# Norm weights folded into the conversion of the feed-forward weights, rows scaled on ScalarE

## The chip, the cores and the metric

The kernel runs on one core of a Trainium2 chip. The metric is the device time of one execution in microseconds (us). The core has five engines, each with a queue of its own that it works off in order: TensorE (PE: matmuls and transposes), VectorE (DVE), ScalarE (ACT), GpSimd (POOL) and SyncE (SP), which here issues the DMAs. An instruction waits at the head of its queue until what it needs is there, and all behind it wait with it.

## The reference

Three stages follow each other. An attention with exponential gates over 2 batches, 8 heads and 768 steps with heads of 40 gives x of 1536 tokens x 320. Then a normed and gated feed-forward layer, then a second feed-forward layer:

```python
def _moe_ref(x, w_gate, w_val, w_out, rms_g):      # 320 -> 1536 -> 320
    rms = np.sqrt(np.mean(x * x, axis=-1, keepdims=True) + 1e-06)
    xn = x / rms * rms_g
    g = xn @ w_gate
    silu = g * (1.0 / (1.0 + np.exp(-g)))
    val = xn @ w_val
    return silu * val @ w_out

def _moe2_ref(x, w_in, w_out):                     # 320 -> 2048 -> 320
    h = x @ w_in
    g = np.maximum(0.01 * h, h)
    return g @ w_out
```

The weights of both layers are 64-bit floats in memory. The kernel reads their bits and makes of each weight a value rounded to the matmul's format and a rest, and multiplies with both.

## The kernel before

The order of all work is one long string, `ORDER`, of some 3000 tokens such as `xn.5` or `a.10`; `play` calls for each the function of that name, and the instructions that it issues go to the ends of the engines' queues. No scheduler changes that order. Only the tokens that the change touches matter here:

- Attention works on 12 tiles T of 128 tokens (6 chunks of 128 steps of each of 2 batches). `dq.T` (`ld_qk`) loads queries and keys in two halves of 40 rows each, `de.T` (`ld_e`) a decay row, spread over 40 rows per half. `arg.T.e` is four exponentials of 128x128 on ScalarE (L359), `y1`, `rec`, `yr` form the attention's output y on VectorE.
- The norm of a tile: `sq.T` (L478) squares y on ScalarE and sums each row; `y2.T.0` (L485) divides by 320 and adds epsilon on VectorE; `y2.T.1` (L487) raises it to -1/2 on GpSimd; `y2.T.2` (L489 to L491) is a Newton step on VectorE in three operations on one column. `xn.T` (`att_xna`, L496) multiplies y by this column and by the norm weights, `gb`, a 128x320 tile into which a DMA spreads the 320 weights. `xc.T` (L500) copies the last 64 columns beside it on ScalarE, `tp.T` (L507) transposes on TensorE, `xh.T` (L511, ScalarE) rounds the result into X, `xl.T` (L515, VectorE) keeps the rest.
- The weights: `wA`, `wR`, `wB` load raw bits; the generators `weight_a`, `weight_r`, `weight_b` are taken a step further by each token `a.k`, `r.k`, `b.k`. The first step makes two halves of the number (L548 on VectorE, L550 on ScalarE), the second puts them together (L552, VectorE) and rounds on ScalarE (L573: 128x512 of key A, L616: two of 64x256 of key R, L627 and L628 of key B), the third takes the difference on VectorE (L575, L619, L630 and L631). Keys A.0 to A.11 and R.0 to R.5 belong to `w_gate` and `w_val`, later ones to the second layer.
- The feed-forward: `U` (L658) is the matmuls of gate `g` and value `v`, `T` the tanh (L685) or, once the attention is over, the silu (L683, with a table load before its first use), `E` (L690) and `M` multiply, `S` and `L` (L706, L712) split the product.
- `close` ends the attention's memory after `tp.11`; keys 8 to 11 of the weights use that memory and are converted only then.

VectorE's `V`, ScalarE's `A`, GpSimd's `G` and SyncE's `Q` are the engines in the code.

Of the kernel before, what the change touches and what calls it, by code (L numbers as in the profile page):

```python
# [50 lines left out]
id.1 id.1 id.1 id.1 z.0 z.1 z.2 did cr id.1 id.1 dfg dig id.1 id.1 id.1 wR.1 dq.0 ms id.1 sf.0.1 sa.0.1 ah sf.1.2 id.1  # L51
sa.1.2 wA.0 co.0.0.1 cv.0.0.1 cl z.3 z.4 z.5 r.1 fa.0.0 arg.0.0 sf.2.6 fa.1.1 uv.0.1 arg.1.1 fa.0.1 sa.2.6 uv.1.2
ux.0.1 co.1.0.1 wR.0 ug.2.6 id.1 co.0.1.2 arg.0.1 r.1 r.0 r.1 r.0 id.1 dn.2 dA.0.2 dq.1 r.0 ev.1.2 ux.2.6 ex.1.2 r.0
r.1 a.0 dn.1 cv.1.0.1 fa.1.0 arg.1.0 dn.0 th.0 eg.2.6 k.0 da.2 ex.2.6 a.0 k.1 qk.0 p.0.0 qk.1 a.0 p.1.0 av.0.0 p.0.1
av.0.1 abs.0 p.1.1 av.1.0 av.1.1 da.3 id.1 mask.2.1 cv.0.1.2 mask.2.0 co.0.2.6 dE.1.2 y1.0 id.1 arg.2.0 a.0 kv.0 abs.1
# [5 lines left out]
co.1.2.6 cv.1.2.6 xl.1 cb.1 y2.2.1 y2.2.2 r.3 qk.4 eq.3 av.3.1 inn.3 dv.1.2 xn.2 arg.4.0 xc.2 tp.2 abs.3 r.3 r.3 c.3
rec.3 dn.5 kv.3 a.4 xh.2 arg.4.1 xl.2 U.0.1.1 p.4.0 k.5 y1.3 da.5 a.4 st.3 U.0.1.0 cb.3 p.4.1 th.5 T.0.1 dn.4 th.4
mask.5.0 wA.3 yr.3 sq.3 a.4 E.0.1 mask.5.1 a.3 arg.5.1 dc.2.6 de.4 r.3 arg.5.0 y2.3.0 a.3 eq.4 M.0.1 av.4.0 av.4.1
inn.4 dq.5 qk.5 y2.3.1 y1.4 p.5.1 U.0.0.0 p.5.0 T.0.0 E.0.0 dv.2.6 U.0.0.1 M.0.0 da.6 mask.6.1 arg.6.1 de.5 wB.0 abs.4
dq.6 a.3 rec.4 mask.6.0 av.5.0 av.5.1 S.0.1 eq.5 y2.3.2 yr.4 S.0.0 inn.5 kv.5 abs.5 b.0 xn.3 rec.5 b.0 sq.4 y2.4.0
y2.4.1 arg.6.0 qk.6 L.0.1 p.6.1 U.0.2.0 p.6.0 U.0.2.1 T.0.2 E.0.2 c.2 y1.5 dq.7 b.0 c.5 st.5 qk.7 yr.5 y2.4.2 c.4 cb.5
sq.5 a.3 k.4 kv.4 id.1 xc.3 tp.3 xh.3 y2.5.0 y2.5.1 dq.8 xn.4 da.7 xc.4 M.0.2 wB.2 U.0.3.0 st.4 cb.4 y2.5.2 c.6 L.0.0
xn.5 xl.3 tp.4 xh.4 xl.4 U.0.3.1 S.0.2 xc.5 T.0.3 tp.5 xh.5 de.6 dn.6 av.6.0 E.0.3 xl.5 av.6.1 wB.3 M.0.3 L.0.2 eq.6
inn.6 abs.6 wA.5 b.0 b.3 U.1.0.0 T.1.0 E.1.0 U.1.0.1 M.1.0 U.1.1.0 da.8 U.1.2.0 b.3 mask.7.0 arg.7.0 p.7.0 dn.7 av.7.0
mask.7.1 arg.7.1 p.7.1 av.7.1 k.7 S.0.3 b.2 L.0.3 de.7 b.2 eq.7 S.1.0 b.2 inn.7 L.1.0 b.2 b.3 b.3 wB.4 rec.6 T.1.2  # L70
# [1039 lines left out]
```

## Time and profile before

| what | value |
|---|---|
| three timed runs | 443.22, 443.83, 448.07 us (median 443.83) |
| the profiled execution | 444.82 us, its span 443.0 us |
| busy: TensorE, VectorE, ScalarE, GpSimd | 429.1 (97%), 367.9 (83%), 280.7 (63%), 104.5 us (24%) |
| mean granted TensorE clock | 0.973 of full speed |
| chain that ended last | TensorE 83%, VectorE 8%, ScalarE 4%, DMA 2% |
| DMA | 42.14 MB, 95 GB/s over the span |

The span is the time from the first to the last instruction of one profiled execution; its own time includes what lies around. The busy shares are averages over stages with different limits; the first 75 us and the stretch from 155 to 175 us, where the change lies, are read apart below.

### The profile page before, as it was taken

How to read it: one execution, taken by the hardware profiler on the slowest of the kernel's cores; microseconds unless marked ns; L12 is line 12 of the kernel's file. 1: busy time of each engine (PE TensorE's matmuls, PEld its weight loads, DVE VectorE, ACT ScalarE, POOL GpSimd, SP SyncE). 2: the span in 40 equal slices, each digit the busy share in tenths (PEclk: the TensorE clock that was granted, in tenths of full speed). 3: DMA queues.
4: the chain of work that ended last, by engine and by line, in shares of the span. 5: the costliest groups of instructions: out<-in, count | busy, mean ns of one | idle time of the engine just before them, and what ended most of it. 6: DMA issues, size and time to landing. Idle time of an engine off the chain costs nothing.

```text
span 443.0 us, 9728 instructions
## 1 busy us (share of the span) xinstructions
PE 429.1 (97%) x3702; PEld 409.6 (92%) x3704; DVE 367.9 (83%) x827; ACT 280.7 (63%) x708; POOL 104.5 (24%) x166
## 2 busy tenths in 40 slices
PE   8897989999999999999999999999999999999997
PEld 4775978999999989999999999999999999999996
DVE  7998999677787758969989999888679897988775
ACT  5777866674664377644565565987866676577442
POOL 4644462431212000463736210010101010110000
PEclk9559999999999999999999999999999999999999
...
GB/s 220 320 304 248 181 323 115 222 169 115 223 2 78 56 77 123 57 84 39 85 2 2 1 0 1 1 9 148 30 34 74 108 48 32 30 31 31 0 2 178
DMA packets 16119, 42.14 MB, mean 95 GB/s; under 512 B 2056, under 2 KB 4040, under 8 KB 16072
## 3 DMA queue, kind: packets, MB, share of 16 engines
...
q8 instruction: 29, 0.48, 0.4%
q14 instruction: 18, 0.15, 0.1%
...
## 4 chain that ended last, share of the span: by engine, by line
PE 83%; DVE 8%; ACT 4%; DMA 2%; issue 2%; SPq 0%; DVEq 0%; ACTq 0%
PE h L808 13%; PE xa L730 10%; PE v L658 8%; PE g L658 8%; PE oa L981 6%; PE oa L979 6%; PE oa L980 6%; PE u L808 6%; PE xw L748 5%; PE h L814 3%; PE h L813 3%; PE s L343 2%; PE o L403 2%; PE u L813 1%; DMA Ab<-A_d 1%
## 5 line engine op out<-in xcount | busy, mean ns | idle before, releaser
L981 PE MATMUL oa<-wB,xl 128*128 128x320 f32 x192 | 59.3, 309 | 0.0
L980 PE MATMUL oa<-wB,xh 128*128 128x320 f32 x192 | 59.3, 309 | 0.0
L979 PE MATMUL oa<-wB,xh 128*128 128x320 f32 x192 | 59.3, 309 | 0.0
L658 PE MATMUL g<-X,wA 128*128 128x384 f32 x256 | 50.3, 341 | 1.8 <-DVE th L690 0.9
L991 DVE TENSOR_TENSOR x<-oa,x 128x320 f32<-128x320 f32 x84 | 39.5, 484 | 14.6 <-PE oa L981 13.9
L658 PE MATMUL v<-X,wA 128*128 128x384 f32 x256 | 49.9, 339 | 0.9 <-ACT X L511 0.7
L658 PEld LDWEIGHTS g<-X,wA 128*128 128x128 f32 x256 | 44.2, 188 | 3.9 <-DVE th L690 1.2
L658 PEld LDWEIGHTS v<-X,wA 128*128 128x128 f32 x256 | 44.5, 188 | 1.5 <-ACT X L511 0.8
L730 PE MATMUL xa<-sh,wB 128*128 128x384 f32 x160 | 45.9, 337 | 0.0
L590 POOL TENSOR_TENSOR sums<-w_A 128x128 f32<-128x128 f32 x8 | 3.9, 487 | 151.6 <-DVE w_A L552 147.0
L981 PEld LDWEIGHTS oa<-wB,xl 128*128 128x128 f32 x192 | 36.1, 188 | 0.1
L980 PEld LDWEIGHTS oa<-wB,xh 128*128 128x128 f32 x192 | 36.0, 188 | 0.0
L979 PEld LDWEIGHTS oa<-wB,xh 128*128 128x128 f32 x192 | 36.0, 188 | 0.0
L808 PE MATMUL h<-X,wA 128*128 128x384 f32 x144 | 32.2, 338 | 0.0
L730 PE MATMUL xa<-sl,wB 128*128 128x384 f32 x96 | 32.2, 336 | 0.0
L955 ACT ACTIVATE c<-c 128x384 f32<-128x384 f32 x48 | 25.2, 524 | 7.2 <-DVE c L852 3.4
L730 PEld LDWEIGHTS xa<-sh,wB 128*128 128x128 f32 x160 | 29.4, 188 | 0.1
L965 DVE TENSOR_TENSOR xl<-c,xh 128x384 fp32r<-128x384 f32 x48 | 26.0, 556 | 1.0 <-ACT xh L960 0.8
L960 ACT CAST xh<-c 128x384 fp32r<-128x384 f32 x48 | 24.3, 513 | 2.9 <-PE oa L980 2.2
L359 ACT ACTIVATE w<-Ab,aeu 128x128 f32<-128x128 f32 x80 | 25.3, 392 | 0.6 <-POOL Ab L363 0.6
L808 PEld LDWEIGHTS h<-X,wA 128*128 128x128 f32 x144 | 25.0, 188 | 0.1
L487 POOL TENSOR_TENSOR sm<-sm,mhalf 128x1 f32<-128x1 f32 x12 | 7.9, 661 | 66.5 <-DVE sm L485 66.5
...
## 6 DMA issues: line engine op xcount, KB each, us to landing
...
```

Of the source, the lines that this page charges most:

```text
L359: A.activation(w[:, j], src, AF.Exp, scale=-1.0, bias=col)
L658: PE.matmul(dst, a, x, start=(i == 0), stop=(i == len(seq) - 1))
L730: PE.matmul(xa, w, x, start=(k == 0), stop=(k == len(seq) - 1))
L748: PE.matmul(xas["w", g, i], a, x, start=(f == NE and k == 0), stop=(f == NF - 1 and k == len(seq) - 1),)
L808: PE.matmul(dst, x, y, start=first and j == 0, stop=j == 2, skip_group_check=not first)
L955: A.activation(t, src, AF.Prelu, alpha=0.01)
L960: A.copy(v["h"], v["t"])
L965: V.tensor_tensor(v["l"], v["t"], v["h"].bitcast(F32), op=ALU.subtract)
L979: PE.matmul(oa, v["h"][:, ts], wb[:, 0:DM], start=m == 0, stop=False)
L980: PE.matmul(oa, v["h"][:, ts], wb[:, DM:], start=False, stop=False)
L981: PE.matmul(oa, v["l"][:, ts], wb[:, 0:DM], start=False, stop=m == 1)
L991: V.tensor_tensor(dst, oas[k, p, i], dst, op=ALU.add)
```

## The change

The norm weights no longer multiply the tokens. Since the rows of `w_gate` and `w_val` meet the same 320 features, each weight row is multiplied by its norm weight when it is converted. A DMA early in SyncE's queue loads `gcol`, 128x3, the norm weights as columns (third column: the last 64, twice); the DMA into `gb` is gone.

- `xn.T` is one ScalarE instruction with the row's scale as a pointer to a column, at the same place of the order.
- The conversion of a key A to 11: the 128x512 rounding becomes two of 128x256, each with its column of `gcol` as scale, and the difference becomes two instructions of 128x256 that multiply and subtract. The pairs of keys R to 5 get the scale too, with no instruction more. Keys of the second layer are as before.
- y lives in three standing tiles of 128x321 whose last column holds epsilon's share; the square runs over 321 columns with a scale, so that its sum is the mean plus epsilon. `y2.T.0` is gone, and `y2.T.2` has two operations instead of three (signs in `rec` are turned for it).
- `ld_qk` and `ld_e` move 48 rows per half instead of 40: 24 DMAs of 192 instead of 160 KB, 20 of 96 instead of 80 KB.
- `A_hl` has room for two chunks (one is filled as before), which makes GpSimd's fill of it longer by 128 columns; three small fills for the epsilon columns stand beside it.

In the order only `dgb` has moved (to the start) and the `y2.T.0` have gone:

```diff
-id.1 id.1 id.1 id.1 z.0 z.1 z.2 did cr id.1 id.1 dfg dig id.1 id.1 id.1 wR.1 ...
+id.1 id.1 id.1 id.1 z.0 z.1 z.2 did cr id.1 id.1 dfg dig dgb id.1 id.1 id.1 wR.1 ...
...
-dA.2.6 eq.2 ux.1.2 co.1.1.2 cv.1.1.2 cv.0.2.6 sq.0 y2.0.0 yr.1 wA.2 kv.1 dgb p.2.0 ...
+... cv.0.2.6 sq.0 yr.1 wA.2 kv.1 p.2.0 ...
```

The code:

```diff
-    gb = attc.tile([128, DM], F32, name="gb")
+    gcol = const.tile([128, 3], F32, name="gcol")
+    Y = [attc.tile([128, DM + 1], F32, name=f"y{n}") for n in range(3)]
...
-        for r in (slice(0, D), slice(64, 64 + D)):
+        for r in (slice(0, 48), slice(64, 112)):
...
     def att_sq(T):
-        A.activation(junk, t["yf"], AF.Square, accum_out=t["sm"][:, 8:9])
+        A.activation(junk, t["yx"], AF.Square, scale=2.0 * DM ** -0.5, accum_out=t["sm"][:, 8:9])
     def att_y2(T, i):
-        if i == 0:
-            V.tensor_scalar(out=v_, in0=ss, scalar1=1.0 / DM, scalar2=1e-6, op0=ALU.mult, op1=ALU.add)
-        elif i == 1:
+        if i == 1:
             G.tensor_tensor(z, v_, mhalf, op=ALU.pow)
         else:
             V.tensor_scalar(out=z2, in0=z, scalar1=z, scalar2=v_, op0=ALU.mult, op1=ALU.mult)
-            V.tensor_scalar(out=z2, in0=z2, scalar1=-0.5, scalar2=1.5, op0=ALU.mult, op1=ALU.add)
-            V.tensor_tensor(z, z, z2, op=ALU.mult)
+            V.tensor_scalar(out=zn, in0=z2, scalar1=3.0, scalar2=z, op0=ALU.subtract, op1=ALU.mult)
     def att_xna(T):
-        V.scalar_tensor_tensor(out=xn[:, 0:DM], in0=t["yf"], scalar=t["z"], in1=gb, op0=ALU.mult, op1=ALU.mult)
+        A.activation(xn[:, 0:DM], t["yf"], AF.Copy, scale=t["z"])
     def memsets():
+        for y in Y:
+            G.memset(y[:, DM:], (DM * 1e-6) ** 0.5)
     def weight_a(key):
-        A.copy(w[:, 0:2], x)
+        for k in range(2):
+            A.activation(w[:, k], x[:, k], AF.Copy, scale=gcol[:, k:k + 1])
         yield
-        V.tensor_tensor(w[:, 2:4], x, w[:, 0:2].bitcast(F32), op=ALU.subtract)
+        for k in range(2):
+            V.scalar_tensor_tensor(
+                out=w[:, 2 + k], in0=x[:, k], scalar=gcol[:, k:k + 1], in1=w[:, k].bitcast(F32), op0=ALU.mult, op1=ALU.subtract,
+            )
     def weight_r(i):
+            if first:
+                A.activation(w[hi, 4], x[hi], AF.Copy, scale=gcol[hi, 2:3])
...
+                V.scalar_tensor_tensor(
+                    out=w[lo, 4], in0=x[hi], scalar=gcol[hi, 2:3], in1=w[hi, 4].bitcast(F32), op0=ALU.mult, op1=ALU.subtract,
+                )
```

What this does to the queues shows at three places. In the rows below a row is one instruction (x2 or x4: so many alike), with its line in the kernel that it belongs to, output and inputs; numbers behind names tell uses of one buffer apart.

VectorE where tile 5 is normalised, before; `xl.3`, `xl.4` and `xl.5` are the three with `tp`:

```order
L712 TENSOR_TENSOR sl_0_1179<-th_0_945,sh_0_1023 128x384
L496 SCALAR_TENSOR_TENSOR xn_1181<-y_1104,sm_1049,gb 128x320
L515 TENSOR_TENSOR X<-tp_1146,X 128x3x128
L515 TENSOR_TENSOR X<-tp_1184,X 128x3x128
L690 SCALAR_TENSOR_TENSOR th_3_1202<-th_3_1202,g_3_1163 128x384
L515 TENSOR_TENSOR X<-tp_1204,X 128x3x128
```

And after:

```order
L490 TENSOR_SCALAR sm_1051<-sm_1051 128x1
L726 TENSOR_TENSOR sl_0_1177<-th_0_947,sh_0_1025 128x384
L514 TENSOR_TENSOR X<-tp_1146,X 128x3x128
L514 TENSOR_TENSOR X<-tp_1182,X 128x3x128
L704 SCALAR_TENSOR_TENSOR th_3_1200<-th_3_1200,g_3_1162 128x384
```

The multiplication by `gb` has left the place ahead of `xl.3`, and the column `sm` has one step fewer.

ScalarE where tile 2 is normalised, before; the four 128x128 are `arg.4.0`, the 64x256 the pair of R.3, `tp` is `xh.2`:

```order
L550 ACTIVATE raw_R_667<-raw_R_667 128x256
L359 ACTIVATE w_0_760<-Ab_571,aeu 128x128 x4
L500 COPY xn_758<-xn_758 128x64
L452 ACTIVATE sm_770<-o_3_681 128x8
L616 CAST wA_773<-w_R_711 64x256
L616 CAST wA_774<-w_R_711 64x256
L511 CAST X<-tp_766 128x3x128
```

And after:

```order
L551 ACTIVATE raw_R_671<-raw_R_671 128x256
L495 ACTIVATE xn_761<-y_108,sm_623 128x320
L360 ACTIVATE w_0_763<-Ab_577,aeu 128x128 x4
L499 COPY xn_761<-xn_761 128x64
L453 ACTIVATE sm_773<-o_3_685 128x8
L623 ACTIVATE wA_776<-w_R_714,gcol 64x256
L623 ACTIVATE wA_777<-w_R_714,gcol 64x256
L510 CAST X<-tp_769 128x3x128
```

The multiplication, `xn_761`, now stands ahead of `arg.4.0` and waits there for VectorE's column `sm`; the pair of R.3 reads `gcol`.

ScalarE just after `close`, before; `raw_A` to `w_A` are the keys A.10 and A.8, `w_R` is R.4, `th` the silu of the first late gate:

```order
L511 CAST X<-tp_2588 128x3x128
L573 CAST wA_2619<-w_A_2296 128x512
L550 ACTIVATE raw_A_1928<-raw_A_1928 128x512
L736 COPY x_92<-xa_0_2_2592 128x3x128
L573 CAST wA_2627<-w_A_2621 128x512
L550 ACTIVATE raw_R_2570<-raw_R_2570 128x256
L550 ACTIVATE raw_B_2498<-raw_B_2498 128x320
L616 CAST wA_2627<-w_R_2630 64x256
L616 CAST wA_2646<-w_R_2630 64x256
L683 ACT_TABLE_LOAD
L683 ACTIVATE th_2_2658<-g_2_2649 128x384
```

And after:

```order
L510 CAST X<-tp_2574 128x3x128
L575 ACTIVATE wA_2605<-w_A_2287,gcol 128x256 x2
L551 ACTIVATE raw_A_1926<-raw_A_1926 128x512
L750 COPY x_92<-xa_0_2_2578 128x3x128
L575 ACTIVATE wA_2615<-w_A_2608,gcol 128x256 x2
L551 ACTIVATE raw_R_2556<-raw_R_2556 128x256
L551 ACTIVATE raw_B_2487<-raw_B_2487 128x320
L623 ACTIVATE wA_2615<-w_R_2620,gcol 64x256
L623 ACTIVATE wA_2636<-w_R_2620,gcol 64x256
L697 ACT_TABLE_LOAD
L697 ACTIVATE th_2_2648<-g_2_2639 128x384
```

The two roundings of 128x512 are two pairs of 128x256, at the same places.

## Rows read from the trace of the kernel before

**Rows 1.** Windows by stage: us, busy time of each engine (instructions), granted clock (PEclk), DMA share, GB/s.

```profile
20.00:35.00 15.00, 13.58 (x180) 9.49 (x173) 14.22 (x39) 10.95 (x36) 5.98 (x9) 0.51 0.88 300
35.00:45.00 10.00, 8.04 (x167) 6.42 (x168) 8.23 (x28) 8.06 (x25) 5.25 (x10) 1.00 0.61 215
45.00:60.00 15.00, 15.00 (x312) 13.55 (x312) 13.98 (x39) 12.51 (x40) 7.43 (x11) 1.00 0.70 235
60.00:75.00 15.00, 12.61 (x239) 11.46 (x239) 14.54 (x29) 8.93 (x28) 7.23 (x9) 1.00 0.49 171
75.00:155.00 80.00, 80.00 (x934) 77.26 (x925) 59.86 (x155) 46.19 (x133) 16.96 (x26) 1.00 0.40 129
155.00:175.00 20.00, 19.11 (x108) 17.92 (x107) 14.24 (x35) 14.57 (x35) 0.00 (x0) 1.00 0.29 99
```

**Rows 2.** TensorE's waits: engine, line, releaser, us in total, times, longest.

```profile
PE tp L507 <- DVE X L515: 1.3, 1, 1.3
...
PE g L658 <- DVE th L690: 0.9, 1, 0.9
...
PE v L658 <- ACT X L511: 0.7, 1, 0.7
...
PE g L658 <- ACT th L683: 0.4, 1, 0.4
PE g L658 <- DVE wA L619: 0.4, 1, 0.4
```

**Rows 3.** Groups by form on VectorE: shapes, busy us, mean ns, idle before.

```profile
L575 DVE TENSOR_TENSOR wA<-w_A,wA 128x512 fp32r<-128x512 f32 x12 | 8.7, 723 | 0.1
...
L496 DVE SCALAR_TENSOR_TENSOR xn<-y,sm,gb 128x320 f32<-128x320 f32 x12 | 8.0, 665 | 0.1
...
L630 DVE TENSOR_TENSOR wB<-w_B,wB 128x256 fp32r<-128x256 f32 x12 | 5.3, 440 | 5.0 <-ACT wB L627 4.7
...
L491 DVE TENSOR_TENSOR sm<-sm 128x1 f32<-128x1 f32 x12 | 2.2, 188 | 0.4
...
L485 DVE TENSOR_SCALAR sm<-sm 128x1 f32<-128x1 f32 x12 | 1.8, 148 | 1.3 <-ACT junk L478 1.3
```

**Rows 4.** Groups by form on ScalarE.

```profile
L359 ACT ACTIVATE w<-Ab,aeu 128x128 f32<-128x128 f32 x80 | 25.3, 392 | 0.6 <-POOL Ab L363 0.6
...
L573 ACT CAST wA<-w_A 128x512 fp32r<-128x512 f32 x12 | 7.4, 615 | 2.2 <-DVE w_A L552 2.1
...
L478 ACT ACTIVATE junk<-y 128x320 f32<-128x320 f32 x12 | 5.6, 466 | 4.2 <-DVE y L472 2.9 <-DVE rG L295 1.2
...
L627 ACT CAST wB<-w_B 128x256 fp32r<-128x256 f32 x12 | 4.9, 404 | 4.4 <-DVE w_B L552 3.2 <-PE tp L507 1.2
...
L594 ACT CAST wA<-w_A 128x128 fp32r<-128x128 f32 x8 | 2.4, 298 | 2.3 <-DVE w_A L552 2.3
```

**Rows 5.** Timeline of VectorE around tile 5's normalisation: start us, us, instruction.

```profile
62.87 2.00 DVE L496 SCALAR_TENSOR_TENSOR xn<-y,sm,gb 128x320 f32<-128x320 f32 x1
64.79 1.01 DVE L515 TENSOR_TENSOR X<-tp,X 128x384 fp32r<-128x384 f32 x2
```

**Rows 6.** Timeline of ScalarE around tile 2's copy.

```profile
39.87 1.27 ACT L359 ACTIVATE w<-Ab,aeu 128x128 f32<-128x128 f32 x4
41.50 0.24 ACT L500 COPY xn<-xn 128x64 f32<-128x64 f32 x1 [0.37 <-DVE xn L496]
```

**Rows 7.** Timeline of ScalarE in the closing stretch.

```profile
157.51 0.62 ACT L573 CAST wA<-w_A 128x512 fp32r<-128x512 f32 x1
158.03 0.68 ACT L550 ACTIVATE raw_A<-raw_A 128x512 f32<-128x512 f32 x1
...
159.47 0.62 ACT L573 CAST wA<-w_A 128x512 fp32r<-128x512 f32 x1 [0.40 <-DVE w_A L552]
...
161.62 0.82 ACT L616 CAST wA<-w_R 64x256 fp32r<-64x256 f32 x2 [0.81 <-DVE w_R L552]
...
163.76 0.49 ACT L683 ACTIVATE th<-g 128x384 f32<-128x384 f32 x1
```

More of the change, by code (lines that the diff above doesn't have):

```diff
@@ L50 @@
 ORDER = """
[L51 to L55, printed above, removed]
@@ L61 @@
[L61 to L65, printed above, removed]
@@ L66 @@
[L66 to L70, printed above, removed]
@@ L161 @@
[L161 to L165 removed]
+id.1 id.1 id.1 id.1 z.0 z.1 z.2 did cr id.1 id.1 dfg dig dgb id.1 id.1 id.1 wR.1 dq.0 ms id.1 sf.0.1 sa.0.1 ah.0
@@ L193, in body @@
     consts_r = attc.tile([128, 272], F32R, name="consts_r")
-    A_hl = attc.tile([48, L], F32R, name="A_hl")
+    A_hl = attc.tile([48, 2, L], F32R, name="A_hl")
     ident, mask = consts[:, 0:128], consts[:, 128:256]
@@ L207, in body @@
     QK = [attc.tile([128, 2, 4, L], F32, name=f"qkt{n}") for n in range(3)]
-    EB = [attc.tile([104, 4, L], F32, name=f"eb{n}") for n in range(3)]
+    EB = [attc.tile([128, 4, L], F32, name=f"eb{n}") for n in range(3)]
+    Y = [attc.tile([128, DM + 1], F32, name=f"y{n}") for n in range(3)]
     Kt = [attc.tile([128, 4, 104], F32, name=f"Kt{b}") for b in range(2)]
@@ L334, in ld_e @@
         for e in range(2):
-            Q.dma_start(out=eb[64 * e:64 * e + D].rearrange("p j l -> p (j l)"), in_=e_v[b, c, e].partition_broadcast(D))
+            Q.dma_start(out=eb[64 * e:64 * e + 48].rearrange("p j l -> p (j l)"), in_=e_v[b, c, e].partition_broadcast(48))
     def att_qk(T, tag="s"):
@@ L456, in att_y1 @@
         num = t["num"]
-        t["y"] = y = work.tile([128, H, D], F32, tag="y", name=f"y{T}")
+        t["yx"] = Y[T % 3]
+        t["y"] = y = Y[T % 3][:, 0:DM].rearrange("p (h d) -> p h d", h=H)
         V.scalar_tensor_tensor(
@@ L465, in att_rec @@
         r = t["sm"][:, 0:8]
-        V.tensor_scalar(out=r, in0=r, scalar1=1.0, scalar2=2.0, op0=ALU.max, op1=ALU.mult)
+        V.tensor_scalar(out=r, in0=r, scalar1=1.0, scalar2=-2.0, op0=ALU.max, op1=ALU.mult)
         V.reciprocal(r, r)
@@ L476, in att_sq @@
         t = st_[T]
-        junk = work.tile([128, DM], F32, tag="junk", name=f"junk{T}", bufs=1)
-        A.activation(junk, t["yf"], AF.Square, accum_out=t["sm"][:, 8:9])
+        junk = work.tile([128, DM + 1], F32, tag="junk", name=f"junk{T}", bufs=1)
+        A.activation(junk, t["yx"], AF.Square, scale=2.0 * DM ** -0.5, accum_out=t["sm"][:, 8:9])
     def att_y2(T, i):
         t = st_[T]
-        ss, v_, z, z2 = (t["sm"][:, i:i + 1] for i in range(8, 12))
-        t["z"] = z
-        if i == 0:
-            V.tensor_scalar(out=v_, in0=ss, scalar1=1.0 / DM, scalar2=1e-6, op0=ALU.mult, op1=ALU.add)
-        elif i == 1:
+        v_, z, z2, zn = (t["sm"][:, i:i + 1] for i in range(8, 12))
+        t["z"] = zn
+        if i == 1:
             G.tensor_tensor(z, v_, mhalf, op=ALU.pow)
```

234 lines of the change are left out of this document (126 added, 108 removed).

## The prediction

> **What bounds the kernel now.** I read the stretches first: busy time of each engine by stage [rows 1]. Up to 35 us TensorE spends part of its time on idle matmuls, with the granted clock at 0.51, the lower of its two levels (1.2 of 2.4 GHz). VectorE is then full (14.22 of 15 us). From 35 us the clock is 1.00. Between 35 and 45 TensorE is busy for 8.04 of 10 us, so 1.96 us are lost; from 45 to 60 nothing is lost; between 60 and 75 it loses 2.39 us while VectorE is busy for 14.54 of 15; from 75 to 155 it loses nothing in 80 us; between 155 and 175 it loses 0.89 us. No step that the change touches runs after 175. So TensorE sets the time, and an edit on ScalarE or VectorE is worth only what it takes from, or adds to, these 1.96 + 2.39 + 0.89 us.
>
> Then TensorE's waits [rows 2], to name the holes. The ones in reach of the change are five: the first `U` step waits 0.7 us for ScalarE's `xh` (L511), `tp.5` waits 1.3 us for VectorE's `xl` (L515), a gate matmul waits 0.9 us for `E` (L690), and in the closing stretch two waits of 0.4 us, for ScalarE's `T` (L683) and for the weight difference L619. TensorE never waits for a DMA.
>
> **Step one, instructions off VectorE.** The multiplication by the norm weights, L496, is 12 instructions, 8.0 us in all, mean 665 ns; L485 is 12 of 148 ns, and one of the three small operations behind the power goes too (L491, 12 of 188 ns) [rows 3]. That is 8.0 + 1.8 + 2.2 = 12.0 us. Against that each of the 12 weight subtractions of 128x512 (723 ns) becomes two of 128x256 (440 ns each), 157 ns more, 1.9 us in all. VectorE's net relief is about 10 us. What lies on the path is another matter: half of the tiles are normalised between 75 and 155 us, where TensorE has no hole, and there the relief buys nothing.
>
> **Step two, instructions onto ScalarE.** The nearest row for the new `xn` on ScalarE is the square of the same tile, 128x320, 466 ns. It has a fixed scale. What a per-row scale costs I take from two 128x128 rows: 392 ns where a pointer to a column is read (L359) and 298 ns where none is (L594): 94 ns. So a new `xn` is 560 ns [rows 4], where VectorE took 544 in the undisturbed case. The Trainium skill, "ScalarE: Activation LUTs", section "What ACT_TABLE_LOAD costs", gives about 93 ns for each pointer operand, and the trace agrees.
>
> For the weights, a 128x512 conversion (615 ns) becomes two of 128x256 (404 ns + 94 each) [rows 4]. Successive instructions overlap: four 128x128 ones with a pointer take 1.27 us, so a step is (1.27 − 0.39) / 3 = 0.29 us [rows 6]; 128 columns more add 128/256 of 615 − 404 = 211 ns, 0.11 us, so a step is 0.40 us and a pair 0.80. The old one had a step of 158.03 − 157.51 = 0.52 us [rows 7]. **Each of the 12 costs +0.28 us**; without overlap it would be 2 x 0.498 − 0.52 = +0.48. Each half of the six remainders gets +0.09 us, 0.18 a pair.
>
> **Step three, where the path gains.** *At 43 us.* Before, VectorE multiplied and ScalarE did `arg.4.0` (four L359, 39.87 to 41.14) meanwhile; it then waited 0.37 us and copied the last columns at 41.50 [rows 6]. Now `xn.2` stands in ScalarE's queue ahead of `arg.4.0`, and behind it `xc.2`. It saves the 0.37 us and costs a step of about 0.46, and if the scale column comes late, everything behind it waits: `arg.4.0`, `xc.2`, the remainder's conversion, `xh.2`. VectorE is by then relieved of two `xn` and of two to three sets of small operations, about 2 x 0.5 + 3 x 0.15 = 1.4 us, of which waits for TensorE in the stretch of the low clock will give some back; I take 0.8 us. Then `xc.2` comes at about the same time, and the relief of VectorE's later queue (one more `xn`) makes `xh.2` 0.35 us earlier. Bounds: a gain of the whole 0.7 us wait, and a loss of 0.9 us if VectorE is no earlier but for this tile's own operations (the scale was there by 41.50 − 0.54 = 40.9, now 0.2 earlier; then 0.46 and 1.27 us, and `xc.2` at 42.4).
>
> *At 65 us.* One `xn`, tile 5's at 62.87, took 2.00 us instead of 0.54, and `xl.3` and `xl.4` stood behind it until 64.79 [rows 5]; `tp.5` waited for them. The pair takes 1.01 us; after its first half, at about 64.79 + 0.6 = 65.4, `tp.5` began, and TensorE's own work had ended 1.3 us before, at 64.1. With `xn.5` gone from VectorE's queue `xl.3` can start at 62.9 and both be done by 64. ScalarE now has `xn.5` (0.46), two operations of 128x384 (`xh.4` and `S.0.2`, some 0.42 each by the 466 ns of 320 columns less the overlap) and the small `xc.5` (0.2) to do, 1.5 us from about 62.7, so `tp.5` can begin at about 64.2: ScalarE's chain and TensorE's own work are late next, side by side. So the wait shrinks by about 1.2 us. I let this contain the 0.35 won before, since `tp.5` then hangs on the chain of tile 5 and not on TensorE's start. Bounds: 0, and 1.3 with the 0.35 on top.
>
> *At 71 us.* VectorE is 2 us ahead of its old queue behind tile 5 and TensorE 1.2 ahead, so 0.8 of the 0.9 us wait for `E` goes; bounds 0 and 0.9. Gains together **2.0 us**.
>
> **Step four, where the path loses.** In the closing stretch the late weights can be converted only after `tp.11`, and ScalarE's queue is the chain: the two conversions at 157.51 and 159.47, the remainder pair at 161.62, then the table load and `T` at 163.76 [rows 7], for which TensorE waits 0.4 us. The first +0.28 us passes through the bits' step L550 and VectorE's L552 to the second conversion; the second is partly hidden by the 0.81 us in which ScalarE waits for the remainder's bits; the pair adds 0.18. I take 0.28 + 0.18 = +0.45 here, and for the wait before L619, with one conversion and one pair ahead of it, 0.42. Sum **+0.87 us**; bounds 0.36 (the pairs alone) and 2 x (0.48 + 0.18) = 1.32, plus one more 0.48 if the second conversion hides nowhere: 1.8.
>
> **Step five, at nothing.** The epsilon column lengthens the square by one column, and takes L485 out of the way from ScalarE to GpSimd. The three fills of it stand at GpSimd's start. The 160 KB broadcast goes, and 24 loads grow from 160 to 192 KB, 20 from 80 to 96 KB, some 0.9 MB more in the run and 0.5 MB more up to 62 us; at the 300 GB/s of [rows 1] that is 1.8 us of transfer that TensorE, which waits for none, doesn't see; if a conversion's data came that late it would cost at most that, and nothing in [rows 2] says so. The Trainium skill ("DMA: Bandwidth & Descriptors", "Why a DMA increments its semaphore by 16 and not by 1") says that a load is spread over the largest number up to 16 that divides its rows: 10 engines for 40 rows, 16 for 48, so that each engine's share falls from four rows to three. No row here shows it; by it the loads would land sooner, and the sum would be the same.
>
> **Sum.** −2.0 + 0.87 = −1.13 us. The profiled run took 444.82 us (span 443.0), so 443.7 by its own time; the median is 0.99 lower, 443.83, and gives **442.7 us**.
>
> **Rivals.** *A, the start gives back all of it.* VectorE is full in both holey stretches, and its relief up to 75 us is some six `xn` (3.3 us and the 1.46 us extra of the slow one) and six sets of small operations (2.0 us), against 6 x 0.16 added: about 5.8 us, more than the holes of 1.96 + 2.39 = 4.35 us. If all holes hang on VectorE, the time is 443.83 − 4.35 + 0.87 = 440.3, and 439.5 if the close loses nothing. A start of TensorE's fast stretch that also comes earlier would take it below 439.4. Against it: in the first stretch idle matmuls fill in, and only 0.7 us of [rows 2] of the first hole names an operation behind the change.
>
> *B, ScalarE becomes the bound (slower).* Place: its queue from 39.9 us. It decides if the scale column of tile 2 comes after 39.9. Then the 0.9 us loss above stands; up to 62 us ScalarE carries six `xn` (6 x 0.46), some five weight pairs (5 x 0.28) and four remainder pairs (4 x 0.18), 4.9 us more, where it has 2.49 us free between 45 and 60 [rows 1]; `tp.5` then waits for `xc.5` instead of `xl.3`, with 0.4 us more than before, and 0.87 is lost at the close: 0.9 + 0.4 + 0.87 = +2.2, **446.0 us**. The skill's page on ScalarE ("Rules for kernel authors") says the same with a rule: multiplications belong on VectorE, which is up to three times as fast; that is for two-byte types, and at 544 against 560 ns the rows show no such ratio here.
>
> *C, the clock.* It is at its lower level until about 35 us, while TensorE does idle and real matmuls in turn. If another rhythm of waits delays its rise by 5 us, the 4 us of matmuls in these (half of 8.04) take twice as long: +4, some 447.8 with nothing else changed.
>
> *D, nothing.* The relief ends in waits for something else, and the close is covered by the 0.89 us that TensorE already loses: 443.8.
>
> **How the numbers follow.** Forecast 0.45, A 0.22, D 0.12, B 0.15, C 0.06. The range of 8 in 10 takes in A's better part and B: 438.8 to 446.1; below it lies A with a shorter start, above it C. A measurement of this kernel can tell about 1%, 4.4 us, from no change: faster than 439.4 has 0.15 (most of A's lower half, with a little of unknown gain), slower than 448.3 has 0.06 (C and the worst of B), within 0.79.
>
> **What would show it.** In the profile after: `tp.5`'s wait gone or below 0.3 us; the 0.9 us wait for L690 gone; in the closing stretch a wait for `T` of about 0.85 instead of 0.4; `xn` on ScalarE at 0.55 to 0.57 us, and pairs of weight conversions at 0.8 us. Wrong would be: a ScalarE queue that stands at `xn.2` waiting for VectorE (B); TensorE's busy share full in 35 to 45 (A); the clock's rise at another time than 35 us (C).

## The result, and the profile after

The changed kernel is slower: 448.61 us median of 20 runs (446.00 to 451.72) against 445.40 us of the kernel before, now also of 20 runs (443.05 to 448.07); the ratio is 1.0077, 95% interval 1.0053 to 1.0102. Forecast were 442.7 us and a range of 438.8 to 446.1. A second measurement of the same kernel, e8 below, gave 1.0084 (1.0045 to 1.0123). Two executions of over 1000 us, one of e15 and one of the kernel before beside e1 to e4, are left out of all figures.

The profiled execution of the changed kernel took 451.57 us with a span of 449.8; it is one of the long ones. Its windows, cut like [rows 1] and shifted by 5 us from the fourth on, with the same columns:

```profile
20.00:35.00 15.00, 13.58 (x203) 9.82 (x196) 14.13 (x37) 13.05 (x42) 5.81 (x9) 0.50 1.05 280
35.00:45.00 10.00, 8.22 (x165) 5.92 (x163) 7.88 (x22) 7.55 (x24) 4.64 (x8) 0.91 0.84 259
45.00:60.00 15.00, 12.66 (x269) 11.43 (x271) 11.73 (x29) 11.19 (x35) 5.77 (x7) 0.91 0.82 226
60.00:80.00 20.00, 19.08 (x273) 17.40 (x273) 15.62 (x34) 12.69 (x40) 9.36 (x15) 0.90 0.47 152
80.00:160.00 80.00, 80.00 (x948) 76.95 (x935) 56.88 (x140) 49.09 (x142) 17.84 (x26) 1.00 0.44 133
160.00:180.00 20.00, 17.81 (x100) 16.54 (x98) 13.40 (x35) 14.67 (x36) 0.00 (x0) 1.00 0.28 98
```

The hole between 35 and 45 us is nearly as large as before (1.78 of 10 us; then it was 1.96). The granted clock of this stretch is 0.91 where [rows 1] shows 1.00, because TensorE's clock rises after 36 us (0.50 from 35 to 36 us, 1.00 from 37), some 2 us later than before. The stretch from 45 to 60 us, full before, now loses 2.34 us and has a granted clock of 0.91 too: some of it at the lower level (1.2 GHz). The stretch that follows loses 0.92 us where it lost 2.39; the closing one loses 2.19 where it lost 0.89. TensorE's waits, to be held against [rows 2]:

```profile
PE o L404 <- issue: 2.3, 1, 2.3
...
PE g L672 <- ACT th L697: 1.1, 1, 1.1
PE tp L506 <- ACT xn L499: 0.9, 1, 0.9
...
PE g L672 <- DVE wA L629: 0.7, 1, 0.7
PE g L672 <- DVE th L704: 0.7, 1, 0.7
...
PE g L672 <- issue: 0.3, 1, 0.3
```

The wait of `tp.5` for `xl` (1.3 us) is gone, that for `E` (L704, before L690) has shrunk from 0.9 to 0.7. New are a wait for `xc.2` (L499) of 0.9 us and one of 2.3 us that names no releaser ("issue"); the closing ones grew from 0.4 and 0.4 to 1.1, 0.7 and 0.3. Around the new hole the windows show what follows it: from 53 to 57 us TensorE does 1.66 us of work, in the next microsecond the clock falls, and for 6 us it works at half speed:

```profile
53.00:57.00 4.00, 1.66 (x81) 1.29 (x83) 2.88 (x10) 2.62 (x9) 0.19 (x1) 1.00 0.71 213
57.00:58.00 1.00, 1.00 (x40) 0.77 (x31) 0.00 (x0) 0.00 (x0) 0.00 (x0) 0.62 0.83 198
58.00:64.00 6.00, 6.00 (x40) 5.70 (x38) 2.67 (x6) 2.93 (x10) 2.65 (x6) 0.50 1.03 336
```

Put side by side, matmul by matmul, the changed kernel's TensorE is 0.15 us behind the old one at 41.5 us, 1.1 at the last transpose of tile 2, 1.0 at 53, 3.5 after the hole, 6.5 at 64.0 when the clock has risen, 5.1 at `tp.5`, 5.4 at 151, and 6.8 from 180 us on. So this one execution lost 1.0 us at the transposes of tile 2, 2.5 in the hole and 3.0 to the clock behind it, won 1.4 at `tp.5`, and lost 1.4 in the close.

The durations came out as worked out from [rows 4]: on ScalarE the new `xn` is 559 ns (560 forecast) and a half of a weight 500 (498). These are groups by form on ScalarE, with busy us and mean ns behind the bar:

```profile
L575 ACT ACTIVATE wA<-w_A,gcol 128x256 fp32r<-128x256 f32 x24 | 10.9, 500 | 2.4 <-DVE w_A L553 2.3
...
L495 ACT ACTIVATE xn<-y,sm 128x320 f32<-128x320 f32 x12 | 6.7, 559 | 2.0 <-DVE sm L490 2.0
```

On VectorE a half of the difference takes 526 ns in the mean where 440 was taken, in the same view (the medians of these two groups are 476 and 424 ns):

```profile
L578 DVE SCALAR_TENSOR_TENSOR wA<-w_A,gcol,wA 128x256 fp32r<-128x256 f32 x24 | 11.6, 526 | 0.0
```

### The profile page after: what moved, and what is told of

The parts are those of the page before. It is cut to its first block, busy times and chain, and to the rows that moved or that the text cites. A ratio compares the mean times of both kernels' runs of the same rounds, so it can differ in the third digit from the quotient of the medians.

```text
span 449.8 us, 9726 instructions
## 1 busy us (share of the span) xinstructions
PE 434.9 (97%) x3702; PEld 413.2 (92%) x3704; DVE 364.0 (81%) x803; ACT 290.2 (65%) x732; POOL 105.1 (23%) x169
## 4 chain that ended last, share of the span: by engine, by line
PE 85%; DVE 8%; ACT 4%; issue 2%; DMA 0%; SPq 0%; DVEq 0%; ACTq 0%
PE h L822 13%; PE xa L744 10%; PE v L672 9%; PE g L672 9%; PE oa L995 6%; PE oa L994 6%; PE oa L993 6%; PE u L822 6%; PE xw L762 5%; PE h L828 2%; PE h L827 2%; PE s L344 2%; PE o L404 2%; PE o L426 1%; PE u L827 1%
## 5 line engine op out<-in xcount | busy, mean ns | idle before, releaser
L672 PE MATMUL g<-X,wA 128*128 128x384 f32 x256 | 51.6, 348 | 2.9 <-ACT th L697 1.1
L672 PEld LDWEIGHTS g<-X,wA 128*128 128x128 f32 x256 | 45.3, 193 | 5.2 <-ACT th L697 1.4
L726 DVE TENSOR_TENSOR sl<-th,sh 128x384 fp32r<-128x384 f32 x32 | 18.9, 591 | 5.5 <-ACT sh L720 5.3
```

The costliest lines, as they stand in the source:

```text
L672: PE.matmul(dst, a, x, start=(i == 0), stop=(i == len(seq) - 1))
```

## The experiments

There were two theories at first. S: the loss is on the engines' queues, `xn.2` ahead of `arg.4.0` and the conversions of the close. P: the 48-row loads hold up the load of TensorE's own code, which makes the 2.3 us hole and the fall of the clock behind it. Each kernel was timed 10 to 12 times beside the kernel before on the same chip. The table gives the ratio to the kernel before with its interval; the mean granted clock over those executions; and the time lost to the clock, (1 - clock) x time, as a mean over them. The kernel before, measured four times with 29 to 35 executions, had a mean clock of 0.970 to 0.972 and lost 12.6 to 13.3 us to it. The last column is a reckoning and not a measured loss: among the 131 executions of the kernel before, one that lost 1 us more by it took 0.4 us more (0.6 among the 88 of the seven measurements of changed kernels with 48 or 50 rows of q and k).

| kernel | rows of q, k / e | ratio | interval | mean clock | lost to the clock, us |
|---|---|---|---|---|---|
| changed (20 executions) | 48 / 48 | 1.0077 | 1.0053 to 1.0102 | 0.968 | 14.3 |
| e8, changed again | 48 / 48 | 1.0084 | 1.0045 to 1.0123 | 0.968 | 14.3 |
| e1, changed, 40 rows | 40 / 40 | 1.0021 | 0.9998 to 1.0044 | 0.973 | 12.2 |
| e3, xn on VectorE | 48 / 48 | 1.0067 | 1.0037 to 1.0096 | 0.971 | 13.1 |
| e4, no scale in the weights | 48 / 48 | 1.0045 | 1.0012 to 1.0078 | 0.969 | 14.1 |
| e5, e1 with xn.2 later | 40 / 40 | 0.9995 | 0.9966 to 1.0024 | 0.973 | 11.8 |
| e10, e5 with 48 rows | 48 / 48 | 1.0048 | 1.0015 to 1.0080 | 0.969 | 14.0 |
| e9, e5 with 50 rows | 50 / 50 | 1.0076 | 1.0047 to 1.0106 | 0.968 | 14.4 |
| e13, e5 with 48 rows of q, k | 48 / 40 | 1.0057 | 1.0029 to 1.0085 | 0.969 | 13.8 |
| e14, e5 with 48 rows of e | 40 / 48 | 1.0003 | 0.9978 to 1.0028 | 0.972 | 12.3 |
| e11, e5, late halves on VectorE | 40 / 40 | 1.0016 | 0.9988 to 1.0045 | 0.971 | 12.9 |
| e2, before with 48 rows | 48 / 48 | 1.0014 | 0.9990 to 1.0039 | 0.969 | 14.0 |
| e7, before, two more loads at 39 us | 40 / 40 | 1.0031 | 0.9999 to 1.0063 | 0.968 | 14.1 |
| e15, before, two more loads at 82 us | 40 / 40 | 1.0008 | 0.9981 to 1.0036 | 0.970 | 13.5 |
| e6, before, epsilon column, tiles by turns | 40 / 40 | 0.9974 | 0.9944 to 1.0004 | 0.974 | 11.7 |
| e12, before, epsilon column | 40 / 40 | 0.9989 | 0.9963 to 1.0015 | 0.970 | 13.3 |

**The rows undone in the changed kernel, and done in the kernel before (e1, e2).**

```diff
 e1, from the changed kernel
-        for r in (slice(0, 48), slice(64, 112)):
+        for r in (slice(0, D), slice(64, 64 + D)):
-  out=eb[64 * e:64 * e + 48]..., in_=e_v[b, c, e].partition_broadcast(48)
+  out=eb[64 * e:64 * e + D]..., in_=e_v[b, c, e].partition_broadcast(D)
 e2, from the kernel before: the other way round
```

> The changed kernel with 40 rows per half again in the loads of q, k and e, all else as changed. Theory P (spread loads): the 48-row loads hold up TensorE's code load, which leaves the hole of 2.34 us before L404 at 54 us and, 0.6 us after it, a second stretch at the lower clock that costs 3.0 us; with 40 rows both are gone, and the time is 445.5 to 446.5 us, the profile without a hole over 1 us between 45 and 62 us. Theory S (ScalarE's queue): the loss is the 0.97 us before tp.2 and the 1.43 us in the closing stretch, and the hole is an accident of one execution; then the time stays at 448 to 449. Both expect the wait before tp.2 to stay at about 0.9 us.

> The kernel before with 48 rows per half in the loads of q, k and e, nothing else changed. Theory P: part or all of the code-load hole comes with the loads alone: 447 to 450 us, against 445.4 of before. Theory S: 445.4 within 1 us, no hole near 54 us.

With 40 rows the changed kernel is at 446.55 us, 1.0021: 0.0056, or 2.5 us, of the loss is gone, near what P expected, and 0.9 us stays, with an interval that holds zero. Its waits show the hole near 54 us gone, and the one for `xc.2` and the closing ones as they were, as S expected; but two waits without a releaser stand earlier, 2.3 us of them before L414 near 34 us:

```profile
PE o L414 <- issue: 2.7, 2, 2.3
...
PE s L344 <- issue: 1.1, 1, 1.1
PE g L672 <- ACT th L697: 1.1, 1, 1.1
PE tp L506 <- ACT xn L499: 0.9, 1, 0.9
...
PE g L672 <- DVE wA L629: 0.7, 1, 0.7
```

So holes without a releaser are not the rows' alone. In the kernel before the rows cost 0.6 us, with an interval that holds zero (445.46 us): less than P expected and inside S's forecast, though its mean clock is near the changed kernel's, 0.969 against 0.968. And one thing stands in e2's profile that no profile with 40 rows of q and k shows: TensorE waits for their load.

```profile
PE s L343 <- DMA qkt<-qk: 1.8, 2, 1.3
```

The same wait is 0.4 us in e8 and 0.3 in e13, and in the five other profiles with 48 or 50 rows of q and k it does not show.

**The multiplication back on VectorE (e3).**

```diff
-        A.activation(xn[:, 0:DM], t["yf"], AF.Copy, scale=t["z"])
+        V.tensor_scalar(out=xn[:, 0:DM], in0=t["yf"], scalar1=t["z"], scalar2=None, op0=ALU.mult)
```

> The changed kernel with the row scaling xn back on VectorE (one operation with the scale column, without norm weights, which stay in the weights' conversion). Theory S: the wait of 0.87 us before tp.2 falls to the 0.3 us of before, the closing stretch keeps its waits of 1.07 and 0.72 us, so 447.3 to 448.0; if the slow multiplication beside GpSimd returns at tile 5, tp.5 waits again and the time is 448.5. Theory P: the hole near 54 us stays, whatever the wait before tp.2 does: 447.5 to 448.5.

447.57 us. That is inside P's range, but P's hole near 54 us is not in the profile; it is inside S's 447.3 to 448.0, too, but S had 448.5 for the case that the slow multiplication came back, and it did. The wait for `xc.2` is gone, and tile 5's slow multiplication is back, as in [rows 5], with a simpler operation that reads no second tile:

```profile
64.89 1.87 DVE L495 TENSOR_SCALAR xn<-y,sm 128x320 f32<-128x320 f32 x1
66.69 1.01 DVE L514 TENSOR_TENSOR X<-tp,X 128x384 fp32r<-128x384 f32 x2
```

`tp.5` waits 0.8 us for it again. So 0.8 of the 1.3 us won at `tp.5` in the changed kernel come from taking this instruction off VectorE; 0.3 go with the epsilon column alone (e6 and e12 below). On the whole the table puts e3 0.4 us under the changed kernel, which the intervals do not tell from nothing.

**No scale in the weights (e4).**

```diff
-        for k in range(2):
-            A.activation(w[:, k], x[:, k], AF.Copy, scale=gcol[:, k:k + 1])
+        A.copy(w[:, 0:2], x)
...
-        first = i < NF // 2
+        first = False
```

> The changed kernel with the conversion of the weights as before (one 128x512 rounding and one difference per key, no scale); the norm weights are left out of the result. Theory S: the two waits of the closing stretch return from 1.07 and 0.72 to about 0.4 each and the 0.30 us one goes, 1.3 us less: 447.2 us; the wait before tp.2 stays. Theory P: as S at the close, but the hole near 54 us stays in most executions; if the time falls to 445.5 or less, the conversions in the start stretch were the cause of the hole.

447.37 us, 0.0032 or 1.4 us under the changed kernel, near the 447.2 of S, though the two intervals overlap. The closing waits are the old ones, to the 0.1 us, and the 0.3 us one is gone:

```profile
PE g L668 <- ACT th L693: 0.4, 1, 0.4
PE g L668 <- DVE wA L629: 0.4, 1, 0.4
```

So the close's 1.3 us belong to the scaled conversions; the waits show it, the time alone would not. P's fall to 445.5 did not come.

**One token moved, with 40 rows (e5).**

```diff
-inn.3 dv.1.2 xn.2 arg.4.0 xc.2 tp.2
+inn.3 dv.1.2 arg.4.0 xn.2 xc.2 tp.2
```

> The changed kernel with 40 rows per half and with one token moved: xn.2 stands behind arg.4.0 instead of ahead of it. Theory S: ScalarE no longer holds arg.4.0 for tile 2's scale, and the wait before tp.2 falls from 0.86 to 0.3 us or less; the closing stretch stays at 1.07, 0.30 and 0.71 us: 445.7 to 446.2 us, 0.5 us under the kernel with 40 rows alone (446.55). Theory P: the same at tp.2; holes of code loads up to 35 us stay, since the loads there are as heavy (DMA share near 1.0).

445.37 us, 0.9995: below S's 445.7 to 446.2, and no longer told apart from the kernel before. The 0.0026 between e1 and e5 are inside the noise of the two measurements; the wait of `tp.2` is gone, and that the profile shows. ScalarE's timeline in the changed kernel, start and length in us:

```profile
40.99 0.56 ACT L495 ACTIVATE xn<-y,sm 128x320 f32<-128x320 f32 x1 [0.91 <-DVE sm L490]
41.46 1.26 ACT L360 ACTIVATE w<-Ab,aeu 128x128 f32<-128x128 f32 x4
42.63 0.23 ACT L499 COPY xn<-xn 128x64 f32<-128x64 f32 x1
```

The timeline of e5's ScalarE:

```profile
39.49 1.26 ACT L360 ACTIVATE w<-Ab,aeu 128x128 f32<-128x128 f32 x4
40.66 0.55 ACT L495 ACTIVATE xn<-y,sm 128x320 f32<-128x320 f32 x1
41.24 0.24 ACT L499 COPY xn<-xn 128x64 f32<-128x64 f32 x1
```

In the changed kernel ScalarE stood for 0.91 us at `xn.2` until VectorE had the scale, at 40.96, and did `arg.4.0` after it; `xc.2` came at 42.63. With the token moved ScalarE fills that wait with `arg.4.0`, and `xc.2` comes at 41.24. e5 has 40 rows, too; e10, below, differs from the changed kernel in this token alone, and its ScalarE shows the same:

```profile
39.12 1.27 ACT L360 ACTIVATE w<-Ab,aeu 128x128 f32<-128x128 f32 x4
40.30 0.55 ACT L495 ACTIVATE xn<-y,sm 128x320 f32<-128x320 f32 x1
40.88 0.24 ACT L499 COPY xn<-xn 128x64 f32<-128x64 f32 x1
```

There `tp.2` still waits 0.35 us for `xn.2` (L495), against 0.87 for `xc.2` in the changed kernel.

**The epsilon column alone (e6, e12).** Two y tiles instead of three, since the norm weights' tile stays; e6 gives them out by turns, so that tile 7 is overwritten before it is read, e12 in an order in which none is.

```diff
+    Y = [attc.tile([128, DM + 1], F32, name=f"y{n}") for n in range(2)]
+        t["yx"] = Y[YB[T]]            # e6: Y[T % 2]
...                                     # square, y2 and rec as in the changed kernel
```

> The kernel before with the epsilon column alone (two standing y tiles of 128x321, square over 321 columns with a scale, y2.T.0 gone, two operations in y2.T.2); norm weights on VectorE, loads and weights as before. Theory S: ScalarE has nothing more, VectorE 12 x 0.3 us less; the closing waits stay at 0.4 and 0.4, tp.5's 1.3 us shrinks by at most 0.3: 444.7 to 445.4 us against 445.4. Theory P: the same, and no more holes than before.

> The kernel before with the epsilon column and the shorter Newton step alone, as the earlier kernel of this kind, but with the two standing y tiles given out so that no tile's rows are overwritten (in the earlier one tile 7's were, and its rows are wrong). All theories: 443.8 to 445 us, 0.5 to 1.5 us under the kernel before; tp.5's wait 1.0 us and the one for L690 0.55 us as in that one, the close as before.

444.02 and 444.62 us, ratios 0.9974 and 0.9989, both intervals with 1 in them. e6 came out below its forecast of 444.7 to 445.4, e12 inside its own. `tp.5`'s wait is 1.0 us in both, 0.3 less, and the close is as before, as expected. It is a part of the change for which no cost shows, and of the kernels that compute the whole result e12 has the lowest ratio; its 0.9989 is not told apart from no change.

**More transfers without the rows (e7, e15).**

```diff
+ dx=lambda n: Q.dma_start(out=x2.rearrange("p a k l -> p (a k l)")[:, n * 1152:n * 1152 + 2 * DM + H * V1], in_=nat[n]),
...
-inn.4 dq.5                          (e7)
+inn.4 dx.2 dx.3 dq.5
...
-wB.7 k.8                            (e15, instead of e7's place)
+wB.7 dx.2 dx.3 k.8
```

> The kernel before with two more loads of 484 KB (into a part of x2 that is written only after 150 us, read by nobody) just ahead of dq.5. Theory P: TensorE's code load that begins at 49.9 us in the kernel before waits behind them by 1.5 to 4 us; TensorE stands at the L403 group near 53 to 56 us with a hole of 1 to 3 us that names no releaser, and in part of the executions its clock falls behind it: 446.5 to 450 us. Theory S or any other that goes by the engines' queues alone: TensorE waits for no data of these loads; at most the six q and k loads behind them come 3 us later, tile 6 is not needed before 66 us, and the time stays within 1 us of 445.4.

e7's two loads were issued at 39.4 us already, since SyncE runs ahead, and not near 47 as meant. There is no hole near 54 us, so P's mark failed; the time is inside its range all the same, 447.04 us (1.0031, interval 0.9999 to 1.0063). The mean clock is 0.968 against 0.970 of the kernel before on the same chip. Neither difference is clear of noise, but together they led to the question whether more transfers act on the clock and not through that one hole.

> The kernel before with the two idle loads of 484 KB issued near 88 us, where TensorE is busy without a gap, instead of near 39 us (447.04 us, mean clock 0.9684, there). Theory L as an effect of transfers on the clock wherever they are: the mean clock falls as it did there, to 0.968 to 0.969, and the time to 446.5 to 447.5. Theory L as an effect in the start alone (there TensorE has gaps and its clock is still to rise): clock 0.970 to 0.972 and 445.0 to 445.9 us, as before.

Issued at 82.0 us, they give 1.0008 with an interval of 0.9981 to 1.0036, and the clock is 0.970: within the range of the kernel before. The median of the runs, 446.04, lies between the forecasts of the two forms. Since neither e7 nor e15 is told apart from no change, the pair does not decide between them.

**Spread or bytes, q and k or e (e8, e9, e10, e13, e14).** All but e8, which is the changed kernel itself, are e5 with other row counts. For the last two and e15 the question had become whether the larger loads act through the clock at large (theory L) or through the holes alone (theory H).

```diff
-        for r in (slice(0, D), slice(64, 64 + D)):
+        for r in (slice(0, 50), slice(64, 64 + 50)):      # e9; e10 and e13: 48
-  out=eb[64 * e:64 * e + D]..., in_=e_v[b, c, e].partition_broadcast(D)
+  out=eb[64 * e:64 * e + 50]..., in_=e_v[b, c, e].partition_broadcast(50)   # e9; e10 and e14: 48
```

> The changed kernel as it is, a second look. Theory P: a hole that names no releaser again, either at the first late code load (31 to 35 us, before L414) or at the one near 54 us; its place and length differ from execution to execution. Theory S: no such hole in this look; the waits before tp.2 (0.87) and in the close (1.07, 0.30, 0.72) are the same to 0.05 us. Time 447.5 to 449.5.

> The changed kernel with xn.2 behind arg.4.0 and 50 rows per half in the loads of q, k and e (more bytes than 48, but a count that 16 does not divide). Theory P as spread: what delays TensorE's code load is the spread over all rings, so 50 rows behave as 40: no hole near 54 us, 445 to 446 us. Theory P as bytes: 50 rows delay it at least as 48 do: a hole of 0.5 to 2.5 us near 53 to 56 us and 446 to 448 us.

> The changed kernel with xn.2 behind arg.4.0 and its 48 rows per half: the pair of the 50-row kernel. Theory P in both forms: a hole of 0.5 to 2.5 us without a releaser near 53 to 56 us, 446.3 to 448 us, 1 to 2 us over the 40-row kernel with the same token moved (445.4). Theory S alone: the rows cost nothing, 445.4 to 446.

> The changed kernel with xn.2 behind arg.4.0 and 48 rows per half in the loads of q and k alone (e at 40). Theory L (load): bytes moved before 62 us keep TensorE's granted clock lower; q and k are 0.58 of the 0.70 MB that the rows add up to there, so 0.8 of the cost of 48 rows: 447.0 to 447.6 us, mean granted clock 0.969 to 0.970 over the executions. Theory H (holes): only executions with a hole near 54 us lose; the six q and k loads just before it are the cause: the same time, with a hole of 0.5 us or more in the profile and the clock as with 40 rows (0.973) in half of the executions.

> The same with 48 rows in the loads of e alone. Theory L: 0.13 MB more before 62 us: 445.5 to 446 us, clock 0.972 to 0.973. Theory H: no hole near 54 us, 445.4.

e8: 448.34 us, with a wait without a releaser of 0.9 us near 55 us instead of 2.3, the others as in the first profile:

```profile
PE g L672 <- ACT th L697: 1.1, 1, 1.1
PE o L404 <- issue: 0.9, 1, 0.9
PE tp L506 <- ACT xn L499: 0.9, 1, 0.9
...
PE g L672 <- DVE wA L629: 0.7, 1, 0.7
```

e10: 446.57 us, by the ratios 0.0053 or 2.4 us over e5 (the medians, of two chips, are 1.2 us apart). e9: 448.77 us, above the ranges of both forms; 50 rows are no cheaper than 48, so P's form in which the spread over the rings is to blame falls. (By the rule of the Trainium skill that the prediction names, from "DMA: Bandwidth & Descriptors", "Why a DMA increments its semaphore by 16 and not by 1", 50 rows go to 10 engines as 40 do and 48 to 16; no run here shows the engines, and the times don't follow their number.) But e9's profile has no hole near 54 us either, and e10's has one of 0.33. e13 has nearly the whole cost, 1.0057, and e14 none, 1.0003 (444.76 us, below both forecasts): the loads of q and k are it. That fits L's bytes (0.58 of 0.70 MB), and of H only that it names q and k: e13's profile has a hole of 1.4 us near 55 us, but it names VectorE's L711 as releaser, where L553, 0.69 us elsewhere, took 1.67.

What e13's profile, 450.60 us, does show is a clock that comes up late. These are its windows from 35 to 45 and from 45 to 60 us, with the columns of [rows 1]; in the first TensorE is busy all the time, at half speed:

```profile
35.00:45.00 10.00, 10.00 (x142) 7.59 (x143) 6.83 (x19) 5.82 (x18) 3.29 (x5) 0.50 0.70 234
45.00:60.00 15.00, 13.39 (x293) 11.21 (x285) 13.62 (x28) 12.42 (x36) 6.67 (x9) 0.94 0.75 200
```

A low clock in this stretch is not the larger loads' alone either: it is 0.67 from 35 to 45 us in the profile of e11 and 0.50 in that of e15, both with 40 rows (448.22 and 446.14 us).

## Why the prediction was wrong

**What bounds the kernel** held: TensorE is full from 80 to 160 us, and what changed lies in the start and the close.

**Where the sum started.** 443.83 us was the median of three executions; 20 of the same kernel have 445.40. So 1.6 of the 5.9 us between forecast and measurement were in the starting value, and even e1, without the larger loads, would have missed the range by 0.5 us.

**Step one** held in kind, but the halves of the difference were mis-sized (526 ns against 440 in the mean, of which some is the surroundings: the unchanged difference of 128x256, L630 before and L644 after, went from 440 to 510).

**Step two** held to some ns: 559 against 560, 500 against 498, a pair of 0.91 us in all, the next instruction 0.81 after its start (163.73 - 162.92), against 0.80.

**Step three, at 43 us, failed in sign.** I took VectorE to be 0.8 us ahead of the old one there, `xc.2` to come at about the same time and `xh.2` 0.35 us earlier. `xh.2` came at 43.87 instead of 42.89, and `xc.2` at 42.63 instead of 41.50, 1.1 us later, a little beyond the bound of 0.9 that I gave for VectorE being no earlier: its L490 ended at 40.96, where the old kernel's scale was there by 40.67 (its L491 ran from 40.51 for 0.16). So VectorE was behind and not ahead; one reason stands in its timeline at 38.17, where L645 took 1.29 us and not the 0.22 of its like in the close. Rival B names this place and this mechanism, and e5 and e10 show it: behind `arg.4.0` the same instruction waits for nothing.

**At 65 us** the prediction was right: `tp.5` has no wait, in every kernel with `xn` on ScalarE, and 0.8 us of it return when it goes back (e3). **At 71 us** 0.8 us were forecast to go: 0.2 went in the changed kernel and in e13, 0.3 in e8, all of it in the seven other kernels with `xn` on ScalarE. But it is gone in e2 and e15 as well, where the multiplication stands on VectorE as before: that the change takes it away is not shown.

**Step four** had the place right and the size too small: 0.87 against 1.1 + 0.3 + 0.7 - 0.8 = 1.3 us. The first wait rose by 0.67 instead of 0.45. The chain from the first conversion after `tp.11` to `T` is 169.84 - 162.09 = 7.75 us, 7.08 before (163.76 - 156.68), and VectorE's timeline after says where the missing 0.2 is:

```profile
164.42 0.69 DVE L553 SCALAR_TENSOR_TENSOR w_A<-raw_A,w_A 128x512 uint32<-128x512 uint32 x1 [0.48 <-ACT raw_A L551]
165.03 1.67 DVE L578 SCALAR_TENSOR_TENSOR wA<-w_A,gcol,wA 128x256 fp32r<-128x256 f32 x4
...
167.05 0.42 DVE L553 SCALAR_TENSOR_TENSOR w_R<-raw_R,w_R 128x256 uint32<-128x256 uint32 x1
```

The conversion's 0.28 us arrive at L553. Behind it VectorE has four halves, 1.67 us, where it had two whole differences, 1.46, before it can do the remainder's bits (167.05): this is 0.2 us that I had left off the chain. The pair of remainders adds 0.21. To shorten ScalarE's part, e11 moved the second half of the late keys' rounding to VectorE:

```diff
+        if key < NE:
             A.activation(w[:, 1], x[:, 1], AF.Copy, scale=gcol[:, 1:2])
+        else:
+            V.tensor_scalar(out=w[:, 1], in0=x[:, 1], scalar1=gcol[:, 1:2], scalar2=None, op0=ALU.mult)
```

> The changed kernel with 40 rows, xn.2 behind arg.4.0, and for keys A.8 to A.11 the second half of the rounding on VectorE, the first on ScalarE. Theory S: ScalarE's chain in the close loses 0.40 us per key and VectorE, idle there for 1.4, 0.2 and 2.7 us, takes it: the wait for T falls from 1.07 to 0.2 to 0.5 us, that before L629 from 0.72 to 0.3 to 0.5, the 0.30 us one goes: 444.0 to 444.6 us, 1.0 us under the same kernel without this (445.4). Rival: VectorE's queue is the chain there, and the difference of the weights comes as late: 445.4.

Its rival held: 445.76 us, no gain, and the wait for `T` is 1.2 us. VectorE's timeline there:

```profile
161.36 0.88 DVE L581 SCALAR_TENSOR_TENSOR wA<-w_A,gcol,wA 128x256 fp32r<-128x256 f32 x2
162.16 0.34 DVE L578 TENSOR_SCALAR wA<-w_A,gcol 128x256 fp32r<-128x256 f32 x1
162.42 0.87 DVE L581 SCALAR_TENSOR_TENSOR wA<-w_A,gcol,wA 128x256 fp32r<-128x256 f32 x2
...
163.65 0.41 DVE L553 SCALAR_TENSOR_TENSOR w_R<-raw_R,w_R 128x256 uint32<-128x256 uint32 x1
```

The remainder's bits come 5.12 us after the first conversion (163.65 - 158.53) instead of 4.96 (167.05 - 162.09): VectorE is the chain there as much as ScalarE.

**Step five failed, and is the largest part of the miss.** I priced the larger loads at nothing because TensorE waits for no transfer. Three pairs of kernels that differ in the rows alone put them at 0.0056, 0.0053 and (q and k against e) 0.0054, 2.4 to 2.5 us, each clear of zero. The reason itself did not hold everywhere: with the larger loads TensorE waits for q and k in e2 (1.8 us), e8 (0.4) and e13 (0.3).

Most of the cost has no wait for a transfer beside it, and part of it goes with the clock. In the pair e10 and e5 the reckoned loss to the clock is 14.0 against 11.8 us, in the pair of the changed kernel and e1 14.3 against 12.2, in the pair e13 and e14 13.8 against 12.3 (this last difference is inside the noise). All seven measurements of changed kernels with 48 or 50 rows of q and k together have a mean clock of 0.969, the four with 40 rows 0.972. But these 1.5 to 2.2 us are not as much time: at the 0.4 to 0.6 us of time for each us that the executions of one kernel show, they come to 0.6 to 1.3 of the 2.4 to 2.5 us, as an estimate. So rival C, with a chance of 0.06, was right in part: TensorE's clock is lower in the mean. It had the trigger wrong: not another rhythm of waits from the edits on the engines (e1 and e5 have these, and a clock of 0.973), but the larger loads. What makes up the rest of their cost is not shown.

Set against the steps: -1.3 at `tp.5`, -0.2 to -0.9 at L704, +1.0 at tile 2 and +1.3 in the close make +0.1 to +0.8 us, and e1 measured 0.0021, 0.9 us; without the 1.0 of tile 2 it is -0.9 to -0.2, and e5 measured -0.0005, -0.2 us. In both the whole 0.9 at L704 is gone, so the low ends are theirs; each measurement is good to 1.0 to 1.3 us, and the sums agree with it no better than that. The rows' 2.5 us on top of the first give 2.6 to 3.3, and the changed kernel measured 0.0077, 3.4 us.

**What stays open** is how the loads act on the clock and on the time. For code loads speaks that of the 14 holes of TensorE of 0.5 us or more without a releaser between 12 and 80 us, in all profiles, 13 end 1.2 to 1.6 us after one of the 16 KB packets of an instruction queue (q8, 29 packets in the run) has landed; the other one, 1.2 us in e7 near 36 us, does not. These are the nine near 34 and near 54 us, with the kernel before beside them, from the trace's DMA records and between TensorE's matmuls, in us:

```
kernel   packet of code   hole of TensorE
changed  53.91 to 55.10   54.25 to 56.59
e2       54.28 to 55.54   55.77 to 56.74
e8       52.85 to 54.15   54.80 to 55.70
e4       52.74 to 54.04   54.87 to 55.45
e1       32.23 to 33.23   32.49 to 34.78
e3       31.92 to 33.12   32.12 to 34.54
e4       31.38 to 32.43   31.57 to 33.94
e14      32.30 to 33.29   32.70 to 34.65
e13      31.27 to 32.41   33.21 to 33.81
before   49.86 to 51.37   none
```

Near 54 us such a hole is in five of the six profiles with 48 rows in all loads (2.3, 1.0, 0.9, 0.6, 0.3 us) and in none of the six with 40 in all and no loads added. But the long holes near 34 us are in e1 and e14, too, which have 40 rows of q and k, and e9 is slow without one, e13 with no longer one than 0.6 us. A fall of the clock behind such a hole stands in the first profile after and, after the 1.2 us hole that ends at 38.3 us, in e11's (1.00 from 36 to 38 us, 0.50 from 39); in e6's it falls after 43 us without one, and in e13 and e15 the clock comes up late with no such hole of over 0.6 us before it. The intervals of e7 and e15 are too wide to say that more transfers cost anything in the kernel before, or only in the start. In the kernel before the rows cost 0.6 us, not 2.4, with a clock as low; why less, no run here tells.
